# A split product's low halves moved from VectorE to GpSimd, with four re-orderings, in an attention, FFN and mixture-of-experts kernel

## The chip, the cores and the metric

The kernel runs on one core of one Trainium2 chip. The metric is the device time of one execution in microseconds (us). PE is TensorE (matmuls; PEld its weight loads), DVE is VectorE, ACT is ScalarE, POOL is GpSimd, and SP is the engine whose queue issues the DMAs.

## The reference, cut to what matters

```python
# q, k, v: [2, 8, 768, 64]: banded attention, a key is kept if it is one of the
# first 8 or at most 95 behind the query, with a bias by distance and head
a = softmax(scale * q @ k.T + bias, where=keep); attn = a @ v      # -> x [1536, 512]
h = x @ w_in                      # [512, 2048]
x = (h * sigmoid(h)) @ w_out      # [2048, 512]
e = argmax(x @ w_gate)            # 8 experts, one for each token
out = softmax(x @ w_gate)[e] * sigmoid(x @ w_output_gate)[e] * (relu(x @ w1[e]) @ w2[e])
```

## The kernel before

The 1536 tokens are 12 blocks of 128, and two blocks are a unit of 256. For exactness each FFN operand is kept as a high half, rounded to a reduced fp32 type that PE reads, and a low half, the rest; a product is three matmul groups (high by high, high by low, low by high). The weights w_in and w_out arrive as words of 64 bits, and three DVE operations on 128x512 (`decode`, L303 to L305) make fp32 of one piece. `spl_w` then takes a cast for the high half (on POOL at L326 in attention, on ACT at L327 later) and a subtraction on POOL for the low one (L333 for w_in, L339 for w_out).

**Attention first.** The first six blocks run in 24 slots of one pair of heads each (`slot_b`): scores on PE (L173), bias and minimum on DVE (L183), exponentials on ACT (L194), transposes on PE (L213), their copies pT out of PSUM (`emit_cp`, by ACT at L220 from slot DQ = 8 to slot 22, by DVE at L219 else), and products with v (L230). At the end of a block the reciprocals of its sums are spread by POOL (L1031), transposed on PE (`emit_rb`, L237), multiplied in by DVE (L242) and split by POOL (L277, L279). One decoding operation stands in each slot from 8 on: `dops` lists 15, for w_in pieces 0 to 2 and w_out pieces 0 and 1. `WPS` lists the slots behind which the five splits stand.

**Then the FFN**, in five chunks of units, `CH=[[0,1],[2],[3],[4],[5]]`, each of 16 steps over the 128-column pieces f of w_in. Chunk zero has two units. A step of it has 24 matmuls of 128x256 (L355, into two PSUM banks, one for each unit), for each unit tanh on ACT into an SBUF tile u with two buffers (L359), on DVE (u+1)*s, written back into the PSUM tile s (L360), a cast on ACT for the high half of g (L363), and on DVE the subtraction for the low half (L364), which is the last to read the bank; and then the 12 matmuls of 128x512 with w_out of two steps earlier (L375 to L377). In chunk zero each step also decodes the w_in piece of two steps later and one w_out piece, whose low half wol is first needed at L377 one step after its subtraction. From chunk one on, the other attention blocks and the gate of finished units run between the steps; the gate's pieces are a list of functions, one in each step: gate1 twice, gate2, gate3 (ranks: six small matmuls into a tile gr, L492 to L494, and DVE work on it) and gate4. The tile gr shares its PSUM bank with the transposed attention output ms (L271), which DVE reads at L279.

**Then the experts** (`moe2`). Their weights come as pieces qr by `load_u` (L578), the rows of an expert's tokens as xw by `load_x` (L688) out of the table xe, into which POOL's indirect DMAs (L515) have scattered them, all loads on SP's queue in the order of the code. ACT and DVE split qr (L583, L584); PE transposes xw (L703) and multiplies (L713, L714).

Each engine takes its instructions in the order of the code, so that a waiting one holds up all behind it.

Of the kernel before, what the change touches and what calls it, by code (L numbers as in the profile page):

```python
# [17 lines left out]
ALU = mybir.AluOpType  # L18
# [5 lines left out]
def kernel(ctx, tc, qk, v, n_global, n_local, w_in, w_out, wg, w1, w2, out):  # L24
# [3 lines left out]
    CH=[[0,1],[2],[3],[4],[5]]  # L28
    PS=bass.MemoryType.PSUM

    SB=24
    LT=3
    DQ=8
    LI=4
    LO=1
    LS=3
    WL=6
    LOPB=(1,2,3)
    WPL=(4,6,8,10,12,14,16,18,20)
    WPS=(12,14,18,22,24)  # L40
    const=ctx.enter_context(tc.tile_pool(name="const",bufs=1,side="left"))
    es_a=ExitStack(); es_m=ExitStack(); es_2=ExitStack()
    attn=es_a.enter_context(tc.tile_pool(name="attn",bufs=1,side="right"))
# [29 lines left out]
    V=nc.vector; A=nc.scalar; G=nc.gpsimd; T=nc.tensor; S=nc.sync  # L73
# [239 lines left out]
    def dec_rest():  # L313
        while half:
            k=half.pop(); r=wraw.pop(k)
            decode(wF[k],r[:,:,0],r[:,:,1],(2,),dct('a'))
    dops=[(k,st) for k in (0,2,4,1,3) for st in range(3)]
    def dec_op():
        if not dops: return
        k,st=dops.pop(0)  # L320
# [24 lines left out]
    s1p={}; gg={}; s2p={}  # L345
# [10 lines left out]
    def s1_ev(u_,f):  # L356

        t=s1p[u_,f]; u=mp.tile([P,256],F32,tag="u",name="u",bufs=2)
        A.activation(out=u,in_=t,func=AF.Tanh,scale=0.5)  # L359
        V.scalar_tensor_tensor(out=t,in0=u,scalar=1.0,in1=t,op0=ALU.add,op1=ALU.mult)  # L360
    def s1_sp(u_,f):
        t=s1p.pop((u_,f)); g=mp.tile([P,2,256],F32R,tag="g",name="g",bufs=6); gg[u_,f]=g
        A.activation(out=g[:,0],in_=t,func=AF.Copy)  # L363
        V.tensor_tensor(out=g[:,1],in0=t,in1=g[:,0],op=ALU.subtract)  # L364
    def s2_mm(c,f):
        if f==0:
            for u in CH[c]: s2p[u]=[ps.tile([P,512],F32,tag=f"s2{2*(u if c==0 else 0)+k}",name=f"s2{k}",bufs=1) for k in range(2)]
# [204 lines left out]
    def load_u(k,i):  # L572

        p,q=divmod(k,4); hf=q//2; e=ereg(p)
        r=m2['a'].tile([P,512],F32,tag="qr",name="qr",bufs=NQR); uqr[k,i]=r
        if q%2==0: src=w1[ds(e,1),i*P:(i+1)*P,hf*512:(hf+1)*512].rearrange("o p f -> p (o f)")
        else: src=w2[ds(e,1),hf*512+i*P:hf*512+(i+1)*P,:].rearrange("o p d -> p (o d)")
        S.dma_start(r,src)  # L578
# [203 lines left out]
    def moe2():  # L782
        late_split()
        early1(0,0)
        run_gates(2)
        early1(0,1)
        logits(NTT-2)
        early1(1,0)
        run_gates(1)
        late1()  # L790
        run_gates(1)
        early1(1,1)
        run_gates(1)
        early2(0)
        late3()
        order(1)
        moe2_open2()
        for k in range(NQR): load_u(4+k//4,k%4)
        load_x(1); load_t(0)
        early3(0,0)  # L800
        early2(1)
        early3(0,1); early3(1,0)
        early3(1,1)
        early4()
        atags[0]=['s1','s1b','a','pv']
        LG=2
        steps=[(p,f) for p in range(NE) for f in range(8)]
        for g in range(len(steps)+LG):
            if g<len(steps):
                p,f=steps[g]  # L810
                def spl():
                    split_u(4*(p+1)+nq[1]//4,nq[1]%4,False); nq[1]+=1
                f1_mm(p,f)
                if f!=2: folds()
                if p+1<NE and f==0: nq[:]=[0 if p else NQR,0]
                ns=(0,0,3,3,3,3,2,2)[f] if p+1<NE else 0
                f1_ev(p,f,spl if ns else lambda: None)
                if p+1==NE and 2<=f<5: flags(f-2)
                if p+1<NE:
                    for _ in range(ns-1): spl()  # L820
                    while nq[0]<min(16,nq[1]+4*(f+1),nq[1]+NQR): load_u(4*(p+1)+nq[0]//4,nq[0]%4); nq[0]+=1
                    if p and f==0: load_x(p+1)
                    if p==0 and f==5:
                        for k,s,n in tiles(0): tail(0,k,xwt[0][:,k,0:1],xwt[0][:,k,1:2])
                    t=tiles(p+1)
                    px=PX
                    if px<=f<px+len(t): prep_x(p+1,t[f-px][0])
            if g>=LG:
                p2,f2=steps[g-LG]
                if p2<NE-1:  # L830
                    f2_mm(p2,f2)
                    if f2==7: f2_ev(p2)
                    continue
                big,last=tiles(p2)
                if f2==7: f2_mm(p2,0,[big])
                f2_mm(p2,f2,[last])
                if f2==7:
                    f2_ev(p2,[last])
                    for k in range(1,8):
                        f2_mm(p2,k,[big])  # L840
                        if k==2: folds()
                    f2_ev(p2,[big])
# [148 lines left out]

    WP={}
    for k,x in enumerate(((0,0,0),(0,0,1),(0,0,2),(0,1,0),(0,1,1),(0,0,3),(0,0,4),(0,1,2),(0,0,5))): WP.setdefault(WPL[k],[]).append(x)
    for k,x in enumerate(((2,0,0),(2,0,1),(2,0,2),(2,1,0),(2,1,1))): WP.setdefault(WPS[k],[]).append(x)
    npv=[SB]; fin=[]
    TB={s:[(0,2*s-2),(0,2*s-1)] for s in range(1,5)}
    for s,hs in ((5,range(3)),(6,range(3,6)),(7,range(6,8))): TB[s]=[(2,h) for h in hs]
# [1 line left out]
    def slot_b(s):  # L999

        ev=[]
        n5,h5=divmod(s-LT-2,4); o5=0<=s-LT-2<SB
        n,hp=divmod(s,4); n1,h1=divmod(s-1,4); n3,h3=divmod(s-LT,4); n4,h4=divmod(s-LT-1,4)
        n2,h2=divmod(s-2,4); cur=s<SB; o1=0<=s-1<SB; o2=0<=s-2<SB; o3=0<=s-LT<SB; o4=0<=s-LT-1<SB
        def a_():
            if s<SB-3: want(min(s+WL,SB-1))
            elif cur: want(s+3)
            if s==0:
                m=two()
                for j in range(2): emit_qk(n,hp,j,m)  # L1010
            if cur: emit_tb(n,hp,0)
            if s+1<SB or o3: m=two()
            if o3: cp[0]=emit_tr(n3,h3,m)
            if s+1<SB:
                for j in range(2): emit_qk(*divmod(s+1,4),j,m)
            if s<3: warm(2)
            if s>=SB and o3: emit_cp(*cp[0],V)
            if o1 and s<SB: emit_exp(n1,h1)
        ev.append(a_)
        def a2():  # L1020
            if cur: emit_tb(n,hp,1)
            if o3 and s<SB: emit_cp(*cp[0],A if DQ<=s<23 else V)
            if o1 and s>=SB: emit_exp(n1,h1)
            if o4: emit_px(n4,h4)
            if o3 and h3==3 and own(n3): emit_rb(n3)
            if o4 and h4==3 and not own(n4): emit_rb(n4)
            if o5 and h5==3 and not own(n5): emit_xx(n5)
            if o2 and h2==3:
                for k in range(2): emit_rs(n2,k)
                r=attn.tile([P,512],F32,tag="t",name="rx",bufs=3)  # L1030
                G.tensor_copy(r.rearrange("p (h d) -> p h d",h=H),rs[n2].to_broadcast([P,H,D])); rs[n2]=r  # L1031
        ev.append(a2)
        def b_():
            if cur: glob_k(n,hp)
            if h4==3 and o4 and own(n4): emit_xx(n4)
            if s==0: table(slice(0,3),(1,))
            if s==1: table(slice(0,3),(2,))
            for d,h in TB.get(s,()): tab_heads(slice(0,2) if d==0 else slice(2,3),slice(0,2) if d==0 else slice(2,3),(h,))
            if hp==3 and 4*(n+1)<SB and cur: load_v(n+1)
        ev.append(b_)  # L1040
        return ev
    cp=[None]
# [41 lines left out]
    with tc.manual_schedule():  # L1084
# [13 lines left out]
        while s<SB:  # L1098
            for k,e in enumerate(slot_b(s)):
                e()  # L1100
                if k==0 and s>=DQ: dec_op()
            if s==6: rows_clear(0)
            s+=1
            for x in WP.get(s,()): w_to(*x)
# [8 lines left out]
        for g in range(len(steps)+LAG):  # L1113
# [23 lines left out]
            if g>=LAG:  # L1137
                c2,f2=steps[g-LAG]
                s2_mm(c2,f2)
                if live and g>=LAG+FB: run_gates(2 if g-(len(CH)-1)*FB in (2,4) else 1)  # L1140
                if f2==FB-1:
                    first_=[lambda u=u: s2_ev(u) for u in CH[c2]]
                    if c2==0: first_.append(lambda: (atags.__setitem__(0,['a','s22','s23']),ded.__setitem__(0,True)))
                    gq[:0]=first_
                    at=len(gq)
                    for u in CH[c2]:
                        seq=[lambda n=n,fn=turn if u in PU else gate1: fn(n) for n in (2*u,2*u+1)]
                        if u in PU: seq=[lambda u=u,fn=fn: fn(u) for fn in (piece1,piece2,piece3,piece4)]+seq+[lambda: None]*2
                        seq+=[lambda u=u,fn=fn: fn(u) for fn in (gate2,gate3,lambda u: gate4(u,1))]
                        for i,fn in enumerate(seq):  # L1150
                            if at+i<len(gq): gq[at+i]=lambda fs=(gq[at+i],fn): [f() for f in fs]
                            else: gq.append(fn)
                        at=len(gq)-(4 if u in PU else 0)
                    run_gates(3 if c2==0 else 1)
                    if c2==len(CH)-2: gq.append(lambda: order(0))
                    if c2==len(CH)-2: gq.append(moe2_open)
# [73 lines left out]
```

## Time and profile before

| | us |
|---|---|
| median of 3 runs | 565.51 (563.87 to 565.89) |
| profiled execution | 565.66 |
| its span | 563.9 |
| PE busy | 550.1 |
| DVE busy | 392.3 |
| ACT busy | 310.1 |
| POOL busy | 147.2 |

The span is what the trace covers, and 1.8 us of the profiled execution lie outside it. Attention of the first six blocks takes until about 42.6 us, chunk zero from there to about 134, the other chunks to about 362, the experts the rest. In the rows below, times count from the span's start.

### The profile page before, as it was taken

To read this page: it belongs to the slowest core of one execution; us is meant where nothing else is said; L and a number is where in the kernel's file an instruction comes from. 1 tells how busy PE (TensorE), PEld (TensorE's weight loads), DVE (VectorE), ACT (ScalarE), POOL (GpSimd) and SP (SyncE) were. 2 spreads that over 40 slices of the span, in tenths; PEclk is the share of its full clock that TensorE was granted. 3 is DMA by queue.
4 is the path that set the end of the run, shared out by engine and by line. 5 is a ranking of instruction groups with operands and counts; after the bars stand their busy time and mean duration, and the time that the engine had idled before them with its cause. 6 is when DMAs were issued, how large, how long until landed. Compare 5 with 4: busy or idle time off the path is not lost.

```text
span 563.9 us, 12050 instructions
## 1 busy us (share of the span) xinstructions
PE 550.1 (98%) x4051; PEld 467.5 (83%) x4051; DVE 392.3 (70%) x1141; ACT 310.1 (55%) x827; POOL 147.2 (26%) x201
## 2 busy tenths in 40 slices
PE   9999999999998999999999999999999999999993
PEld 4668898888887888888889889888888888888882
DVE  6996999996587767565635457647674966977950
ACT  7994344442644656444632426727655766867740
POOL 4884644344141431213101010210010110010011
PEclk9999999999999999999999999999999999999998
DMA  7886477796575765864593349319673867768500
GB/s 224 269 258 217 152 210 240 241 305 203 181 181 143 194 168 137 181 170 132 113 186 115 95 131 360 110 59 343 225 224 135 270 212 238 253 216 282 158 21 22
DMA packets 87531, 106.76 MB, mean 189 GB/s; under 512 B 35980, under 2 KB 50316, under 8 KB 87460
## 3 DMA queue, kind: packets, MB, share of 16 engines
q1 hardware_dynamic: 84980, 99.25, 59.6%
q0 software_dynamic: 2192, 6.39, 3.1%
q8 instruction: 34, 0.56, 0.4%
q14 instruction: 37, 0.30, 0.2%
q10 hardware_dynamic: 288, 0.26, 0.1%
HBM read 87.14 MB, written 17.66 MB: 186 GB/s over the span
## 4 chain that ended last, share of the span: by engine, by line
PE 87%; DVE 5%; ACT 3%; DMA 1%; POOL 1%; issue 1%; SPq 1%; POOLq 0%; ACTq 0%; DVEq 0%
PE s L355 24%; PE s L375 8%; PE s L376 7%; PE s L377 7%; PE h L713 7%; PE y L746 4%; PE h L714 4%; PE y L748 4%; PE y L747 4%; PE xy L173 3%; PE pv L254 2%; PE h L719 2%; PE y L742 2%; PE y L741 1%; PE xm L703 1%; DMA xw<-xe 1%
## 5 line engine op out<-in xcount | busy, mean ns | idle before, releaser
L355 PE MATMUL s<-xT,wi 128*128 128x256 f32 x1152 | 152.9, 284 | 0.4 <-DVE g L364 0.4
L355 PEld LDWEIGHTS s<-xT,wi 128*128 128x128 f32 x1152 | 146.5, 190 | 8.0 <-DVE g L364 3.3
L360 DVE SCALAR_TENSOR_TENSOR s<-u,s 128x256 f32<-128x256 f32 x96 | 39.8, 426 | 64.4 <-ACT u L359 64.4
L359 ACT ACTIVATE u<-s 128x256 f32<-128x256 f32 x96 | 35.3, 379 | 87.0 <-PE s L355 86.4
L375 PE MATMUL s<-woh,g 128*128 128x512 f32 x192 | 78.4, 408 | 0.0
L584 DVE TENSOR_TENSOR uq<-qr,uq 128x512 fp32r<-128x512 f32 x112 | 74.5, 689 | 3.0 <-ACT uq L583 1.0
L376 PE MATMUL s<-woh,g 128*128 128x512 f32 x192 | 75.7, 394 | 0.0
L583 ACT ACTIVATE uq<-qr 128x512 fp32r<-128x512 f32 x112 | 66.6, 625 | 0.9 <-DMA qr<-in_w_dram 0.9
L670 POOL DMA_INDIRECT out_dram<-y,ixt x17 | 18.9, 1113 | 155.2 <-ACT y L759 113.4
L364 DVE TENSOR_TENSOR g<-s,g 128x256 fp32r<-128x256 f32 x96 | 39.2, 421 | 18.3 <-ACT g L363 14.4
L363 ACT ACTIVATE g<-s 128x256 fp32r<-128x256 f32 x96 | 35.9, 380 | 28.6 <-DVE s L360 28.5
L194 ACT ACTIVATE t<-t,mx 128x256 f32<-128x256 f32 (+1 forms) x96 | 46.1, 487 | 0.5 <-DVE mx L183 0.5
L375 PEld LDWEIGHTS s<-woh,g 128*128 128x128 f32 x192 | 36.3, 189 | 6.9 <-issue 1.8
L376 PEld LDWEIGHTS s<-woh,g 128*128 128x128 f32 x192 | 36.3, 189 | 5.1
L377 PE MATMUL s<-wolr,g 128*128 128x512 f32 x128 | 39.8, 392 | 0.0
L201 POOL TENSOR_TENSOR hl<-t,hl 128x512 f16<-128x512 f32 (+1 forms) x18 | 19.5, 1085 | 75.5 <-ACT g L363 31.6
L726 DVE TENSOR_TENSOR h<-h,hs 128x192 f32<-128x192 f32 (+5 forms) x56 | 20.9, 372 | 25.3 <-ACT hs L725 25.2
L746 PE MATMUL y<-uq,hh 128*128 128x512 f32 (+1 forms) x88 | 36.7, 417 | 0.0
L747 PE MATMUL y<-uq,hh 128*128 128x512 f32 (+1 forms) x88 | 34.6, 393 | 0.0
L748 PE MATMUL y<-uq,hh 128*128 128x512 f32 (+1 forms) x88 | 34.6, 393 | 0.0
L728 ACT ACTIVATE hh<-h 128x192 fp32r<-128x192 f32 (+5 forms) x56 | 19.7, 352 | 26.4 <-DVE h L726 15.9
L731 DVE SCALAR_TENSOR_TENSOR hh<-h,hh 128x128 fp32r<-128x128 f32 (+4 forms) x88 | 23.3, 295 | 13.2 <-ACT hh L728 13.2
(279 smaller groups left out, 1065.4 us busy)
## 6 DMA issues: line engine op xcount, KB each, us to landing
qr<-in_w_dram SPq DMA_DIRECT2D x128, 256.0 KB, 4.3
wolr<-wlo_d SPq DMA_DIRECT2D x64, 256.0 KB, 3.3
wiraw<-in_w_in_dram SPq DMA_DIRECT2D x16, 512.0 KB, 4.0
wraw<-in_w_out_dram SPq DMA_DIRECT2D x13, 512.0 KB, 3.8
ring<-in_qk_dram SPq DMA_DIRECT2D x22, 256.0 KB, 4.1
xe<-xe SPq DMA_DIRECT2D x7, 792.0 KB, 6.2
wlo_d<-wol SPq DMA_DIRECT2D x16, 256.0 KB, 2.6
xw<-xe SPq DMA_DIRECT2D x15, 264.0 KB, 5.0
```

Source lines behind the costliest of these rows:

```text
L194: A.activation(out=t[:,j,:ce],in_=t[:,j,:ce],func=AF.Exp,scale=-1.0 if 4*n<SB else 0.125,bias=mx[n][:,h:h+1],accum_out=ss[n][:,h,0:1])
L355: T.matmul(t,w[:,ww,kc,:],x[:,xx,kc,:],start=(k==0),stop=(k==11)); k+=1
L360: V.scalar_tensor_tensor(out=t,in0=u,scalar=1.0,in1=t,op0=ALU.add,op1=ALU.mult)
L375: T.matmul(o,g[u][:,0,sl],wh,start=(f==0),stop=False)
L376: T.matmul(o,g[u][:,1,sl],wh,start=False,stop=False)
L377: else: T.matmul(o,g[u][:,0,sl],wl,start=False,stop=(f==FB-1))
L583: A.activation(out=t[:,0],in_=r,func=AF.Copy)
L584: (G if (i%2 if pool is None else pool) else V).tensor_tensor(out=t[:,1],in0=r,in1=t[:,0],op=ALU.subtract)
L713: for kc in range(KC): T.matmul(t[:,:2*W],uq[4*p+2*(f//4),kc][:,0,s],xwT[p,kc][:,:,:W],start=(kc==0),stop=False)
L746: T.matmul(o,hi,w[:,0],start=(f==0),stop=False)
L747: T.matmul(o,g[:,z:z+n],w[:,0],start=False,stop=False)
L748: T.matmul(o,hi,w[:,1],start=False,stop=(f==7))
```

## The change

It has four parts (line numbers of the kernel after are two to five above those of before).

1. Only the nine decoding operations of w_in pieces 0 to 2 are left in attention, in slots 8 to 18 without 11 and 15 (`DQS`), with their three splits (`WPS`). The w_out pieces 0 and 1 are decoded in steps 0 and 1 of chunk zero, as the others are. In slots 11, 15 and 20 (`CPV`) the pT copies are DVE's.
2. In chunk zero, (u+1)*s is written to the SBUF tile u in place, the cast reads it there, and the subtraction for the low half is POOL's, not DVE's. Other chunks keep what they had.
3. The ranks of unit 1 come one step later.
4. The second expert's rows xw are asked for after four of the eight qr loads.

```diff
+    DQS=(8,9,10,12,13,14,16,17,18)
+    CPV=(11,15,20)
-    WPS=(12,14,18,22,24)
+    WPS=(12,15,20)
...
-    dops=[(k,st) for k in (0,2,4,1,3) for st in range(3)]
+    dops=[(k,st) for k in (0,2,4) for st in range(3)]
...
-        V.scalar_tensor_tensor(out=t,in0=u,scalar=1.0,in1=t,op0=ALU.add,op1=ALU.mult)
+        o=u if u_ in CH[0] else t; s1p[u_,f]=o
+        V.scalar_tensor_tensor(out=o,in0=u,scalar=1.0,in1=t,op0=ALU.add,op1=ALU.mult)
...
-        V.tensor_tensor(out=g[:,1],in0=t,in1=g[:,0],op=ALU.subtract)
+        (G if u_ in CH[0] else V).tensor_tensor(out=g[:,1],in0=t,in1=g[:,0],op=ALU.subtract)
...
-        for k in range(NQR): load_u(4+k//4,k%4)
-        load_x(1); load_t(0)
+        for k in range(NQR):
+            load_u(4+k//4,k%4)
+            if k==3: load_x(1)
+        load_t(0)
...
-            if o3 and s<SB: emit_cp(*cp[0],A if DQ<=s<23 else V)
+            if o3 and s<SB: emit_cp(*cp[0],A if DQ<=s<23 and s not in CPV else V)
...
-                if k==0 and s>=DQ: dec_op()
+                if k==0 and s in DQS: dec_op()
...
-                        seq+=[lambda u=u,fn=fn: fn(u) for fn in (gate2,gate3,lambda u: gate4(u,1))]
+                        seq.append(lambda u=u: gate2(u))
+                        if u==1: seq.append(lambda: None)
+                        seq+=[lambda u=u,fn=fn: fn(u) for fn in (gate3,lambda u: gate4(u,1))]
```

On DVE, one steady step of chunk zero stands like this before: three decoding operations (dct and wt are the decoder's tiles, wraw raw w_out, wiraw raw w_in), the two units' products, the two subtractions into g, and the next decoding.

```order
L303 TENSOR_SCALAR dct<-wraw 128x512
L304 SCALAR_TENSOR_TENSOR dct<-wraw,dct 128x512
L360 SCALAR_TENSOR_TENSOR s_1493<-u,s_1493 128x256
L360 SCALAR_TENSOR_TENSOR s_1506<-u,s_1506 128x256
L364 TENSOR_TENSOR g<-s_1493,g 128x256
L364 TENSOR_TENSOR g<-s_1506,g 128x256
L305 SCALAR_TENSOR_TENSOR wt<-wraw,dct 128x512
```

And after the change:

```order
L305 TENSOR_SCALAR dct<-wraw 128x512
L306 SCALAR_TENSOR_TENSOR dct<-wraw,dct 128x512
L363 SCALAR_TENSOR_TENSOR u<-u,s_1493 128x256
L363 SCALAR_TENSOR_TENSOR u<-u,s_1506 128x256
L307 SCALAR_TENSOR_TENSOR wt<-wraw,dct 128x512
```

The two subtractions have gone, and no DVE instruction reads the bank s behind the product.

On POOL, steps 1 to 3 of chunk zero stand like this before (xT is the split of an attention block, rx the spread reciprocals, upper the first tile of the gate's constants).

```order
L277 CAST xT<-xn 128x4x128
L279 TENSOR_TENSOR xT<-xn,xT 128x4x128
L326 CAST woh<-wt 128x512
L339 TENSOR_TENSOR wol<-wt,woh 128x512
L1031 COPY rx<-rs 128x512
L333 TENSOR_TENSOR wi<-wt,wi 128x512
L277 CAST xT<-xn 128x4x128
L279 TENSOR_TENSOR xT<-xn,xT 128x4x128
L333 TENSOR_TENSOR wi<-wt,wi 128x512
L388 MEMSET upper 128x128
```

And after the change:

```order
L281 TENSOR_TENSOR xT<-xn,xT 128x4x128
L367 TENSOR_TENSOR g<-u,g 128x256 x2
L1036 COPY rx<-rs 128x512
L367 TENSOR_TENSOR g<-u,g 128x256 x2
L341 TENSOR_TENSOR wol<-wt,woh 128x512
L335 TENSOR_TENSOR wi<-wt,wi 128x512
L367 TENSOR_TENSOR g<-u,g 128x256 x2
L279 CAST xT<-xn 128x4x128
L281 TENSOR_TENSOR xT<-xn,xT 128x4x128
L341 TENSOR_TENSOR wol<-wt,woh 128x512
L335 TENSOR_TENSOR wi<-wt,wi 128x512
L391 MEMSET upper 128x128
```

Each step has got two subtractions, ahead of the weights' own, and the casts of woh have left the queue.

On PE, unit 1's ranks in chunk one stand like this before, right behind the w_out matmuls of a step and ahead of the next step's w_in matmuls (s_2145 and s_2146 are the unit's sums, geb the chosen experts).

```order
L376 MATMUL s_2146<-woh,g 128x512
L377 MATMUL s_2145<-wolr,g 128x512
L377 MATMUL s_2146<-wolr,g 128x512
L492 LDWEIGHTS upper
L492 MATMUL gr<-geb,upper 128x8
```

And after the change:

```order
L379 MATMUL s_2146<-woh,g 128x512
L380 MATMUL s_2145<-wolr,g 128x512
L380 MATMUL s_2146<-wolr,g 128x512
L357 MATMUL s_2694<-xT,wi 128x256 x12
L175 MATMUL xy<-ring_76 128x256 x4
```

The w_in matmuls follow directly, and the ranks come behind that step's own w_out matmuls.

## Rows read from the trace of the kernel before

**Rows 1.** The page: PE's busy time, the chain by engine, one group of instructions.
```profile
PE 550.1 (98%) x4051; PEld 467.5 (83%) x4051; DVE 392.3 (70%) x1141; ACT 310.1 (55%) x827; POOL 147.2 (26%) x201
PE 87%; DVE 5%; ACT 3%; DMA 1%; POOL 1%; issue 1%; SPq 1%; POOLq 0%; ACTq 0%; DVEq 0%
...
L364 DVE TENSOR_TENSOR g<-s,g 128x256 fp32r<-128x256 f32 x96 | 39.2, 421 | 18.3 <-ACT g L363 14.4
```

**Rows 2.** Chain of waits, 59 to 138 us: w_in matmuls (start, us, what).
```profile
59.72 2.87 PE s L355 x24
65.34 2.87 PE s L355 x24
...
93.43 3.05 PE s L355 x24
...
134.31 1.43 PE s L355 x12
```

**Rows 3.** Waits, 42.6 to 138 us: total us, times, longest.
```profile
PEld s L355 <- DVE g L364: 3.3, 8, 0.7
```

**Rows 4.** Timeline of one step (start, us, engine, line, tiles; [idle before <- releaser]).
```profile
118.35 1.30 POOL L339 TENSOR_TENSOR wol<-wt,woh 128x512 fp32r<-128x512 f32 x1 [2.30 <-ACT woh L327]
...
119.17 0.69 DVE L305 SCALAR_TENSOR_TENSOR wt<-wiraw,dct 128x512 int32<-128x512 int32 x1
...
121.22 0.75 DVE L360 SCALAR_TENSOR_TENSOR s<-u,s 128x256 f32<-128x256 f32 x2
...
122.10 0.76 DVE L364 TENSOR_TENSOR g<-s,g 128x256 fp32r<-128x256 f32 x2
122.58 0.19 PEld L355 LDWEIGHTS s<-xT,wi 128*128 128x128 f32 x1 [0.39 <-DVE g L364]
```

**Rows 5.** Busy time by stretch, PE, PEld, DVE, ACT, POOL; clock, DMA, GB/s.
```profile
23.50:30.00 6.50, 6.50 (x88) 4.22 (x86) 6.20 (x25) 6.50 (x27) 6.18 (x9) 1.00 1.00 337
...
93.40:134.30 40.90, 40.90 (x255) 35.62 (x255) 37.22 (x69) 17.21 (x41) 17.13 (x14) 1.00 0.82 264
```

**Rows 6.** Timeline of PE, start of chunk zero's third step.
```profile
53.05 3.13 PE L355 MATMUL s<-xT,wi 128*128 128x256 f32 x24 [0.42 <-DVE g L364]
```

**Rows 7.** Timeline of POOL, steps 2 to 4 of chunk zero.
```profile
58.72 0.61 POOL L277 CAST xT<-xn 128x512 fp32r<-128x512 f32 x1 [1.25 <-DVE xn L242]
...
62.75 0.21 POOL L388 MEMSET upper<- 128x128 bf16 x1
...
65.98 1.30 POOL L339 TENSOR_TENSOR wol<-wt,woh 128x512 fp32r<-128x512 f32 x1
```

**Rows 8.** Timeline of POOL and DVE: subtractions in chunk one.
```profile
163.03 0.69 POOL L201 TENSOR_TENSOR hl<-t,hl 128x256 f16<-128x256 f32 x1
...
166.63 1.53 DVE L201 TENSOR_TENSOR hl<-t,hl 128x512 f16<-128x512 f32 x1
```

**Rows 9.** Timeline of PE and DVE around unit 1's ranks.
```profile
180.10 0.68 DVE L279 TENSOR_TENSOR xT<-ms,xT 128x512 fp32r<-128x512 f32 x1
...
180.84 0.17 PE L492 MATMUL gr<-geb,upper 128*128 128x8 bf16 x1 [1.67 <-DVE xT L279]
...
187.82 0.43 DVE L360 SCALAR_TENSOR_TENSOR s<-u,s 128x256 f32<-128x256 f32 x1 [2.14 <-ACT u L359]
```

**Rows 10.** Timeline of POOL, SP's queue and PE where the second expert begins.
```profile
377.32 0.97 POOL L515 DMA_INDIRECT xe<-xr,gdi  x1 [2.04 <-DMA xe<-xr,gdi]
378.37 4.45 SPq L578 DMA_DIRECT2D qr<-in_w_dram  x8
383.34 2.00 SPq L688 DMA_DIRECT2D xw<-xe  x3
...
389.46 0.63 PE L703 MATMUL xm<-ident,xw 128*128 128x128 f32 x4 [0.45 <-DMA xw<-xe]
```

**Rows 11.** Timeline of attention: a pair of pT copies, and PE's wait for POOL.
```profile
34.49 0.68 ACT L220 ACTIVATE pT<-xy 128x256 f32<-128x256 f32 x2
...
41.05 0.42 PEld L237 LDWEIGHTS rb<-ident,rx 128*128 128x128 f32 x4 [0.37 <-POOL rx L1031]
```

More of the change, by code (lines that the diff above doesn't have):

```diff
@@ L993 @@
     for k,x in enumerate(((0,0,0),(0,0,1),(0,0,2),(0,1,0),(0,1,1),(0,0,3),(0,0,4),(0,1,2),(0,0,5))): WP.setdefault(WPL[k],[]).append(x)
-    for k,x in enumerate(((2,0,0),(2,0,1),(2,0,2),(2,1,0),(2,1,1))): WP.setdefault(WPS[k],[]).append(x)
+    for k,x in enumerate(((2,0,0),(2,0,1),(2,0,2))): WP.setdefault(WPS[k],[]).append(x)
     npv=[SB]; fin=[]
```

## The prediction, made before the result was known

> **What bounds the kernel now.** I read the page's busy times and the chain of waits first. PE is busy 550.1 us of the span's 563.9 and is 87% of the chain [rows 1]. Its clock is granted in full, 1.00, which is the level of 2.4 GHz [rows 5]. So nothing can be won but PE's gaps, at most 563.9 - 550.1 = 13.8 us, and each part of the change has to be set against the gap that it is aimed at. The other engines cost only where one of them makes PE wait.
>
> The longest stretch of such gaps is chunk zero. Along the chain, a step (from one start of the 24 w_in matmuls to the next) takes 65.34 - 59.72 = 5.62 us at first, but from 93.43 on the seven steps to 134.31 take 40.88, that is 5.84 each [rows 2]. The waits of that stretch name one releaser, the DVE subtraction L364: 3.3 us in 8 waits of PE's loads [rows 3]. The timeline of one late step shows it directly: DVE runs the products, then the subtractions from 122.10, and PE's next load starts as they end the first bank, having stood for 0.39 [rows 4]. DVE is busy 37.22 of 40.90 us there [rows 5], and the rest is gaps of a few hundredths between its instructions. A step's DVE work is six decoding operations of 0.69, two products (0.75) and two subtractions (0.76) [rows 4], 5.65 us, or 5.84 with the gaps: DVE is the bound by two tenths of a microsecond in each step, and falls behind until PE's lead is used up at 93.43.
>
> **Part 2, chunk zero: the sum's first two terms.** The subtractions leave DVE, 0.76 in a step, and it has 5.84 - 0.76 = 5.1 us of work in PE's 5.62. The bank is free once the product has been written to u, earlier than before by cast and subtraction. So steps should run at PE's own 5.62: 13 x 5.62 = 73.1 against 134.31 - 59.72 = 74.6 us, **1.5 us won**. The third step's start at 53.05 waits 0.42 for the same subtraction [rows 6]; that should go too: **0.4 won**.
>
> What the six decoding operations of w_out add in steps 0 and 1 (6 x 0.69 = 4.1 us on DVE) lies in the first three steps, where DVE loses the subtractions of 0.76 in each and has gaps; their low halves come in the same pattern as piece 2's, a step before use. I cost that at nothing.
>
> The new work is 32 subtractions on POOL. No row has this form exactly. The nearest is POOL's own subtraction of a 128x256 tile, 0.69 [rows 8], with an f16 result; from above bounds the 128x512 one of 1.30 [rows 4], from below half of it, 0.65. I take 0.69, the same size. POOL then has 1.30 + 1.30 (the weights' two) + 2 x 0.69 = 4.0 us in a step of 5.62. The cast reading SBUF rather than PSUM is ACT's, which is busy 17.21 of 40.90 [rows 5]: nothing.
>
> The new wait is tanh's: u has two buffers, POOL reads them last, and behind a waiting tanh on ACT stand the casts, on which DVE's and POOL's work and then PE hang. In a steady step POOL is done with u by about 4.5 us into the step, and the next tanh comes at 5.62 + 1.4: slack 2.5. The tight place is the gate's constants on POOL, from 62.75 to the start of L339 at 65.98, 3.2 us [rows 7]. I follow POOL by the new order from step 2, in estimates from these durations. Its two subtractions end at about 58.9, close to where the attention block's cast starts now, 58.72; that cast and its subtraction (0.61 + 1.30) end at 60.8, the two weights' (2.6) at 63.4, the constants at 66.6, step 3's subtractions (1.4) at 68.0, and the low half of w_out piece 2 at 69.3. PE needs that last one in step 4, behind 24 w_in matmuls and eight with w_out: step 3 starts at 59.72 - 0.42 = 59.3, and 59.3 + 5.62 + 2.87 is 67.8; the twelve w_out matmuls share 5.62 - 2.87 = 2.75, eight of them 1.8, so 69.6. The margin is 0.3 us; tanh of step 4 waits about 1 us, PE does not, and POOL has caught up two steps later. So I cost it at nothing, narrowly.
>
> Here a rule speaks against the part. The row has POOL at 0.69 for the size. The Trainium skill, "GPSIMD Engine Reference", section "4.1 Engine selection", says that elementwise work belongs on VectorE and that GpSimd is about twice as slow with two inputs. By that, an estimate from the rule and the 0.42 mean of DVE's subtraction [rows 1] would be 0.84, the low half would be 4 x 0.15 - 0.3 = 0.3 late, once, and the whole sum 3.9 where it is 4.2 by the row.
>
> **Part 3, ranks of unit 1.** PE waits 1.67 us at 180.84 because the ranks' tile shares a bank with the transposed block that DVE reads at L279, 180.10 to 180.78 [rows 9]. One step later the bank has long been read; the w_in matmuls, which need nothing of it, go first. The six small matmuls cost the same wherever they stand. DVE's work on the ranks then waits at its queue's head for PE; behind it stands the next product, before which DVE has 2.14 idle [rows 9], more than the few short operations take. What is late next would be the pT tiles of that stretch, which DMA transposes bring behind DVE's own splits and which PE needs a step later; I reckon a few tenths to spare. **1.7 won**, and as little as nothing if PE meets these instead (rival B).
>
> **Part 4, rows of the second expert.** PE waits 0.45 for xw at 389.46 [rows 10]. Eight qr loads ahead of it take SP 4.45, 0.56 each; four fewer bring xw 2.2 us sooner, past the need. The rows must lie in xe by then: the last scatter runs to 377.32 + 0.97, and the one before kept POOL waiting for 2.04 until it had landed [rows 10], so by about 380.3, and xw would now be asked for at 383.34 - 2.2 = 381.1. The four qr loads that now stand behind come 2.0 later [rows 10]; by its order ACT takes their pieces only after that, and should it wait, at most those 2.0 less its lead are lost. **0.5 won**.
>
> **Part 1, attention.** In the stretch shown ACT is full (6.50 of 6.50), and so is PE [rows 5]. Three pairs of pT copies, 0.68 for two that overlap [rows 11], leave ACT, some 2 us, for DVE, in slots in which DVE loses a decoding operation of 0.69. So ACT's relief is 2 us at the most, but PE shows next to no gap there into which it could go, and near the end it is the block's way over POOL that sets the time: PE waits 0.37 for it at 41.05 [rows 11]. In the new order that way's first step, L242, stands behind two pairs of copies on DVE, about where it begins now. I take **0.1 won**, a part of that one gap; the range is from 0.4 lost (the gap twice as long) to 0.8 won (near half of ACT's relief reaches PE, rival C).
>
> **Sum.** 1.5 + 0.4 + 1.7 + 0.5 + 0.1 = 4.2 us. Against the profiled execution, 565.66 - 4.2 = 561.4. The median of the runs is 565.51, 0.15 lower, so 561.3 us.
>
> **The rivals.**
> *A. POOL is late once, at the constants (563.9).* PE's waits for L364 go as reckoned, but POOL's subtraction costs near its upper bound. At 1.29 a POOL step is 5.2, still under 5.62, but at the constants four subtractions are each 0.6 longer: 2.4 less the margin of 0.3, and half a microsecond from the step before, some 2.6 us late once. 561.3 + 2.6 = 563.9. For it: no row has the fp32r result with this size. Against: the 128x512 form with that result is 1.30, twice 0.65, so size and not type sets it.
> *B. The ranks' wait is replaced (562.9).* If the transposes or another DVE product come as late as the bank did, part 3 gives nothing or little, and 561.3 + 1.6 = 562.9. For it: chunk one is the place where DVE, SP and PE are all close. Against: after the waits of that step DVE has 2.14 idle.
> *C. Attention gains more (560.5).* If the three copies shorten the whole way from slot 11 on, 0.6 to 0.8 more. For it: ACT is busy without a gap. Against: the wait for POOL.
> *D. Slower: POOL becomes chunk zero's bound (570.1).* DVE's subtraction L201 took 1.53 in a stretch in which POOL worked too [rows 8], where DVE's subtraction of that size at L279 took 0.68 [rows 9]: 0.85 more. If POOL's subtractions lose as much beside DVE's steady work, they cost 0.69 + 0.85 = 1.54 to 1.30 + 0.85 = 2.15; in the middle, 1.85, a POOL step is 2.6 + 3.7 = 6.3, and 13 steps take 81.9 rather than 73.1: 561.3 + 8.8 = 570.1. It decides from (5.62 + 0.32 - 2.6) / 2 = 1.67 each, where the loss in 13 steps eats the 4.2. Against: POOL's 1.30 at 118.35 ran beside DVE's L305 at 119.17, and both took what they take elsewhere [rows 4]. The Trainium skill, "SBUF — State Buffer", section "SBUF: two separate sides", has the two engines lock each other out only when DVE has two SBUF inputs or a two-port mode; L201 has two, and no DVE operation of chunk zero has, so by that page D does not come.
> *E. Part 2's gaps hide another bound,* as the weights' splits that now stand behind the subtractions on POOL: then the steps stay at 5.84, and 1.5 + 0.4 are lost, 563.2.
>
> **How the numbers follow.** Forecast 0.57 (560.8 to 562.0), A 0.12, B 0.11, C 0.09, E 0.06, D 0.05. The range takes in C and, above, B, E and A: 559.9 to 564.0, leaving out D and the tails. A measurement of this kernel tells about 0.5% (2.8 us) from no change: faster means under 562.7, slower over 568.3. Faster: the forecast with C, 0.66, and the milder half of B and the mildest of A, 0.07, make 0.73. Same: the rest of A and B with E, 0.22. Slower: D, 0.05.
>
> **What the profile after would show.** Steps of chunk zero at 5.62 throughout, no wait of PE for L364 or its POOL successor, and 128x256 subtractions on POOL of about 0.7; tanh waiting for POOL about 1 us in step 4 alone; no wait ahead of the ranks, and none in place of it at the next pv; xm without a wait; attention's end within half a microsecond of 42.6. I am wrong if POOL's subtraction is well over 0.8, if PE waits for wol in step 4, or if the 1.7 us return elsewhere in chunk one.

## The result: slower, 571.84 us

The changed kernel takes 571.84 us (median of 4 runs, 570.56 to 572.41) where the kernel before takes 565.06 (median of 4): 1.0118 times as long, interval 1.0092 to 1.0145, some 6.7 us. The prediction was 561.3, with 559.9 to 564.0 as its range; it is wrong in sign.

The page of the kernel after, its busy times and the engines of its chain:

```profile
PE 551.8 (97%) x4051; PEld 469.8 (82%) x4051; DVE 385.1 (68%) x1115; ACT 312.1 (55%) x823; POOL 168.7 (30%) x231
...
PE 81%; DMA 5%; DVE 5%; ACT 2%; POOL 2%; SPq 2%; issue 2%; POOLq 0%; DVEq 0%; ACTq 0%
```

Against [rows 1] DVE has given work to POOL as planned, and yet PE's share of the chain has fallen from 87% to 81%, while DMA's, POOL's and SP's queue's, 1% each before, have grown. Of DMA's 5%, 1% is wgs; 3% are qr loads in the chain between 340 and 400 us. What is new for PE, the waits from 60 to 85 us of the kernel after say (engine, line, what it waited for: us, times, longest):

```profile
PEld s L380 <- POOL wol L341: 6.4, 1, 6.4
PE s L380 <- POOL wol L341: 6.0, 1, 6.0
POOL wgb L405 <- DMA wgs<-in_wg_dram: 5.9, 1, 5.9
```

One stall, in step 4 of chunk zero. POOL stood 5.9 us for wgs, the gate's weights, and PE stood 6.0 for the low half wol that POOL makes behind it. The chain of waits of that stretch shows the whole way (start, us, what):

```profile
61.34 1.26 POOL wol L341
62.60 0.02 issue
62.62 0.33 SPq L343
...
62.99 0.93 SPq L416
...
63.97 0.61 SPq L291
...
64.63 0.50 SPq L295
...
65.17 6.42 DMA wgs<-in_wg_dram
...
72.92 1.41 POOL g L367 x2
74.33 1.23 POOL wol L341
...
75.60 2.07 PE s L380 x4
77.67 4.44 PE s L357 x24
...
84.87 2.87 PE s L357 x24
```

It is read from the top: POOL finishes the low half of w_out piece 1, and only then can SP issue its write to DRAM (L343). Behind that write, on SP's queue, stand a clearing of xe (L416), two raw weights (L291, L295), and then wgs at 65.17, which lands 6.42 later. Before the change the same queue stood like this (timeline of SP, kernel before):

```profile
42.94 0.33 SPq L341 DMA_DIRECT2D wlo_d<-wol  x1
...
47.53 0.33 SPq L341 DMA_DIRECT2D wlo_d<-wol  x1
...
52.10 0.55 SPq L400 DMA_DIRECT2D wgs<-in_wg_dram  x1
```

and after it (timeline of SP, kernel after):

```profile
55.54 0.33 SPq L343 DMA_DIRECT2D wlo_d<-wol  x1
...
62.62 0.33 SPq L343 DMA_DIRECT2D wlo_d<-wol  x1
...
65.17 0.64 SPq L403 DMA_DIRECT2D wgs<-in_wg_dram  x1
```

The two writes are 12.6 and 15.1 us later because w_out pieces 0 and 1 are decoded and split later, and wgs, whose place in the code hasn't changed, is 13.1 us later. Before, POOL read it first 12.6 us after its issue, and did not wait (timeline of POOL, kernel before):

```profile
64.71 0.24 POOL L402 CAST wgb<-wgs 128x64 bf16<-128x64 f32 x1
```

Little of those 12.6 us was to spare. When it landed the trace of before doesn't show; in those of parts 2 and 3, each alone, where SP's queue is in the order of before, wgs landed 9.6 and 9.2 after its issue, 1.6 and 3.6 us ahead of POOL's first reading.

The last rows of the chain show a second price. Four w_out matmuls take 2.07 where they take 0.91 elsewhere, and 24 w_in matmuls 4.44 for 2.87: 2.7 us more. The stretches of busy time of the kernel after name it (PE, PEld, DVE, ACT, POOL, then the granted clock):

```profile
69.00:72.00 3.00, 0.58 (x3) 0.15 (x1) 0.00 (x0) 0.00 (x0) 0.26 (x2) 1.00 0.52 166
...
77.70:79.00 1.30, 1.30 (x8) 1.30 (x8) 1.16 (x3) 0.45 (x1) 1.30 (x2) 0.50 0.96 321
...
82.20:85.00 2.80, 2.80 (x15) 2.35 (x14) 2.30 (x4) 1.74 (x4) 2.02 (x3) 1.00 0.42 124
```

PE had been idle for 6 us, and came back at a granted clock of 0.50, the 1.2 GHz level, until about 81.1. So the stall cost 6.0 + 2.7 = 8.7 us.

By stages of the two traces: the stretch from the first w_in matmul of chunk zero to the first of chunk one is 91.6 us before (42.69 to 134.31) and 98.2 after (42.90 to 141.07), so 6.6 more, that is 8.7 lost and about 2.2 won. From there to the first eh matmul, which opens the experts, 0.7 is won: 1.8 at the ranks, where PE no longer waits, less 1.1 at the end of chunk four, where ACT stood 0.5 for a late qr; of the other profiles only that of parts 2 and 3 alone loses as much as 0.7 there. From there to the last yf matmul, the last product of the experts, 0.2 is lost.

### The profile page after: what moved, and what is told of

Its sections match the earlier page's. It is cut to its first block, busy times and chain, and to the rows that moved or that the text cites. A ratio compares the mean times of both kernels' runs of the same rounds, so it can differ in the third digit from the quotient of the medians.

```text
span 570.3 us, 12053 instructions
## 1 busy us (share of the span) xinstructions
PE 551.8 (97%) x4051; PEld 469.8 (82%) x4051; DVE 385.1 (68%) x1115; ACT 312.1 (55%) x823; POOL 168.7 (30%) x231
## 4 chain that ended last, share of the span: by engine, by line
PE 81%; DMA 5%; DVE 5%; ACT 2%; POOL 2%; SPq 2%; issue 2%; POOLq 0%; DVEq 0%; ACTq 0%
PE s L357 20%; PE s L378 6%; PE h L716 6%; PE s L380 6%; PE s L379 6%; PE y L749 4%; PE xy L175 4%; PE y L750 4%; PE y L751 4%; PE h L717 4%; DMA qr<-in_w_dram 3%; PE pv L256 2%; PE h L722 2%; PE px L232 2%; PE y L745 1%
## 5 line engine op out<-in xcount | busy, mean ns | idle before, releaser
L357 PEld LDWEIGHTS s<-xT,wi 128*128 128x128 f32 x1152 | 148.9, 193 | 5.4 <-issue 0.3
L363 DVE SCALAR_TENSOR_TENSOR s<-u,s 128x256 f32<-128x256 f32 x64 | 27.3, 426 | 56.0 <-ACT u L361 55.9
L367 DVE TENSOR_TENSOR g<-s,g 128x256 fp32r<-128x256 f32 x64 | 27.0, 421 | 16.6 <-ACT g L366 14.8
L366 ACT ACTIVATE g<-s 128x256 fp32r<-128x256 f32 x64 | 24.3, 380 | 22.6 <-DVE s L363 22.5
L716 PE MATMUL h<-xwT,uq 128*128 128x448 f32 (+5 forms) x144 | 32.5, 347 | 0.0
```

The lines of the kernel that those rows point to most:

```text
L357: T.matmul(t,w[:,ww,kc,:],x[:,xx,kc,:],start=(k==0),stop=(k==11)); k+=1
L716: for kc in range(KC): T.matmul(t[:,:2*W],uq[4*p+2*(f//4),kc][:,0,s],xwT[p,kc][:,:,:W],start=(kc==0),stop=False)
```

## The experiments

Theory Q, after the result: SP stands for the moved writes, wgs is late, POOL's queue stands for wgs, PE for wol. Rival P: POOL, with the new subtractions, could not have brought wol in time in any case, and the wgs wait only fills time that POOL's load would have cost. All comparisons are with the kernel before on the same chip, where it took 565.6 to 565.8. The first four expectations count from the 565.06 above, so that they stand 0.6 too low.

**Wgs loaded early.** The whole change, with one DMA moved from step 3 of chunk zero into attention's slot 20:

```diff
-        S.dma_start(wgs,wg.rearrange("(k p) e -> p k e",p=P))
...
             if s==6: rows_clear(0)
+            if s==20: S.dma_start(wgs,wg.rearrange("(k p) e -> p k e",p=P))
```

> The whole change, but the load of the gate's weights wgs is issued in attention's slot 20, ahead of the two wol writes on SP's queue, not at step 3 of chunk zero. Theory Q (queue): the loss is SP standing for the moved wol writes, so that wgs lands late (71.6 us), POOL stands 5.9 us for it at the gate's constants and PE 6.0 us for wol of piece 2 behind that, with the clock down afterwards (2.7 us). Then POOL no longer waits for wgs, PE waits at most 0.3 us for wol in step 4, the clock stays at 1.00, and the time is 565.1 - 1.5 - 0.4 - 1.7 = 561.5 us, 561.0 to 562.3. Rival P (POOL's load): with the new subtractions POOL cannot bring wol in time after the constants anyway. Then PE still waits 2 us or more in step 4, and the time is 563.5 to 567 us.

Measured: 563.05 us, 0.9955 times before (0.9939 to 0.9971), 2.6 us faster. One 32 KB transfer issued earlier turns the change from 1.2% slower to 0.45% faster. Its chain in steps 3 to 6:

```profile
59.40 2.87 PE s L357 x24
...
65.02 2.89 PE s L357 x24
67.91 0.72 POOL g L367
68.63 1.26 POOL wol L341
...
69.93 1.21 PE s L380 x4
71.14 2.87 PE s L357 x24
...
76.76 2.87 PE s L357 x24
```

A wait of 0.2 us for wol is left (step 4 takes 71.14 - 65.02 = 6.12, half a microsecond over 5.62), all other steps from 3 on are at 5.62. P expected 2 us or more, so Q holds, with P true to half a microsecond: this is the narrow place that the prediction followed on POOL. The time lies 0.8 above Q's range: 0.6 of that is the base, the rest less than step 4's half microsecond.

**Part 1 alone** (the decoding moved, three pT copies on DVE, subtractions still on DVE):

```diff
+    DQS=(8,9,10,12,13,14,16,17,18)
+    CPV=(11,15,20)
-    WPS=(12,14,18,22,24)
+    WPS=(12,15,20)
...
-    dops=[(k,st) for k in (0,2,4,1,3) for st in range(3)]
+    dops=[(k,st) for k in (0,2,4) for st in range(3)]
...
```

> Part 1 alone (w_out pieces 0 and 1 decoded in chunk zero, three pT copies on DVE); the subtractions stay on DVE. Q: the wol writes are late on SP here too, wgs lands at about 71 us, POOL stands for it about 6 us, and wol of piece 2 comes one POOL subtraction (1.3 us) later at about 74; PE waits 4 to 5 us for it and runs at half clock for some 4 us, 2.7 us: 565.1 + 4.5 + 2.7, less up to 1.5 that DVE gains back while PE stands: 570.8 us, 569.5 to 572.5. P: no new subtraction on POOL, so no stall: 565 us, 564.3 to 565.8.

Measured: 574.26 us, 1.0154 (1.0132 to 1.0176). The stall is here without any new work on POOL (waits, 60 to 85 us):

```profile
POOL wgb L404 <- DMA wgs<-in_wg_dram: 5.3, 1, 5.3
...
PE s L379 <- POOL wol L341: 4.6, 1, 4.6
```

So part 1 makes the stall by itself, which P can't explain. The time is above Q's range by 1.8 us, 0.6 of it the base; besides, at the ranks of unit 1, which this kernel still has a step early, PE waits 1.7 and then comes back at a lower clock, which costs 1.5 and of which more below.

**Part 1 alone, wgs early**, to take the stall away from it:

```diff
...
-        S.dma_start(wgs,wg.rearrange("(k p) e -> p k e",p=P))
...
+            if s==20: S.dma_start(wgs,wg.rearrange("(k p) e -> p k e",p=P))
```

> Part 1 alone with wgs loaded early. Q: the stall of part 1 alone goes (no wait of PE for wol over 0.5 us in step 4, clock 1.00): 8 us less than part 1 alone, 565.9 us (564.8 to 566.8). Rival: the late writes and reads of wol themselves hold PE up: 568 us or more.

Measured: 569.28 us, 1.0066 (1.0047 to 1.0085). The wait for wol is gone, but not all of the loss. The time is the rival's, 2.5 above Q's range, but not for the rival's reason: PE waits for no wol or wolr in chunk zero. The chain of chunk zero shows the first part of the loss:

```profile
59.72 2.87 PE s L357 x24
65.33 3.02 PE s L357 x24
71.10 3.10 PE s L357 x24
76.95 3.10 PE s L357 x24
```

From 65.33 on the 24 matmuls take more than 2.87, and the steps go to 5.85; before, this began only at 93.43 [rows 2]. With the six decoding operations, 4.1 us of work, DVE's lead is used up five steps sooner, and chunk zero takes 1.1 us more. Alone, part 1 is a loss; only without the subtractions on DVE is it hidden. Another 1.5 us lie behind unit 1's ranks, again with a lower clock.

**Part 2 alone** (product into u, subtraction on POOL):

```diff
...
+        o=u if u_ in CH[0] else t; s1p[u_,f]=o
...
+        (G if u_ in CH[0] else V).tensor_tensor(out=g[:,1],in0=t,in1=g[:,0],op=ALU.subtract)
```

> Part 2 alone (product to SBUF, the low halves' subtraction on POOL in chunk zero); w_out pieces 0 and 1 decoded in attention as before, so SP's queue is as before. Q: wgs is there in time (issued at about 52), no PE wait in step 4 over 0.3 us, steps of chunk zero at 5.62, 128x256 subtractions of 0.7 on POOL: 565.1 - 1.9 = 563.2 us, 562.6 to 564.0. P: PE waits about 2 us in step 4: 565 us or more.

Measured: 564.47 us, 0.9984 (0.9968 to 1.0000): 0.9 us won by the ratio, 0 to 1.8, in the forecast's range only with the base put right. P's mechanism isn't there, as PE has no wait in step 4. In its trace chunk zero takes 89.4 us (42.07 to 131.49) and not 91.6: 2.2 won there, a little over the 1.9 forecast. What is missing in its time is seen at the ranks (stretches with the granted clock, as above, and PE's timeline):

```profile
177.00:178.70 1.70, 0.28 (x7) 0.28 (x7) 1.36 (x5) 0.13 (x2) 1.15 (x1) 1.00 0.84 269
178.70:180.00 1.30, 1.30 (x8) 1.30 (x8) 1.02 (x8) 0.21 (x1) 0.00 (x0) 0.55 0.29 78
180.00:181.50 1.50, 1.50 (x8) 1.27 (x9) 0.33 (x1) 0.13 (x1) 0.48 (x2) 0.50 1.02 195
```
```profile
178.41 0.17 PE L493 MATMUL gr<-geb,upper 128*128 128x8 bf16 x1 [1.67 <-DVE xT L279]
...
178.57 2.70 PE L355 MATMUL s<-xT,wi 128*128 128x256 f32 x12
181.20 1.62 PE L173 MATMUL xy<-ring 64*128 64x256 f32 x8
```

The same place in the kernel before:

```profile
179.00:180.90 1.90, 0.23 (x4) 0.15 (x4) 1.75 (x7) 0.55 (x2) 1.06 (x1) 1.00 0.75 222
180.90:182.50 1.60, 1.60 (x18) 1.55 (x17) 1.09 (x8) 0.21 (x1) 0.09 (x1) 1.00 0.45 130
```

The wait is the 1.67 us of [rows 9], but after it the clock is at 0.50, and the next matmuls take 2.70 and 1.62 where in the kernel before they take 1.66 and 1.13. In the traces of this kernel, of part 1 alone and of part 1 with wgs early, the step behind the ranks takes 6.2 to 6.3 us where it took 4.7: 1.5 us more. In the kernel before the clock stays at 1.00 over the same wait, and in part 4 alone over one of 1.18.

**Part 3 alone** (unit 1's ranks a step later):

```diff
...
+                        if u==1: seq.append(lambda: None)
...
```

> Part 3 alone (ranks of unit 1 one step later). As forecast: no wait of PE at the ranks, none in its place: 565.1 - 1.7 = 563.4 us, 562.9 to 564.0. Rival: another wait takes its place at the next products with v: 564.5 to 565.5 us.

Measured: 564.20 us, 0.9978 (0.9965 to 0.9991), 1.3 us won by time (0.5 to 2.0), between the forecast's range and the rival's, and in the forecast's with the base put right. In the trace the wait is gone, and from chunk one's first w_in matmul to the first eh it takes 225.9 us, before 227.9. But a new wait has come, at a product with v, as the rival had it, a quarter as long (timeline of PE):

```profile
197.19 0.76 PE L254 MATMUL pv<-vpr,pT 128*128 128x64 bf16 x20 [0.43 <-DMA pT<-hl]
```

The other profiles with part 3 have at most 0.3 there, that of the whole change under 0.1. Nor is the 2.0 a measure by itself: the trace of part 4 alone, whose code is the same up to the experts, has a wait of 1.18 at the ranks, and their step takes 5.5 us in it, where it takes 6.3 in the kernel before and 4.0 here.

**Part 4 alone** (the second expert's rows after four loads):

```diff
...
+            if k==3: load_x(1)
...
```

> Part 4 alone (the second expert's rows after four qr loads). As forecast: no wait of PE at xm and none in its place, 0.5 us won: 565.2 us where the kernel before takes 565.65; from the first eh matmul to the last yf one 188.0 us, before 188.5. Rival (a new wait takes its place): the four qr loads that now stand behind land later, ACT stands for them, its split of xw comes late and PE waits 0.3 us or more for it: nothing won, 565.5 to 566.0, that stretch 188.5 to 188.8.

Measured: 566.50 us, 1.0013 (0.9998 to 1.0028): nothing won. The rival's mechanism holds; the time is 0.5 above its range. The trace, of the fastest of the 12 runs (563.62), has no wait at xm, the transposes of xw, but these (timeline, 380 to 405 us):

```profile
386.32 1.28 ACT L583 ACTIVATE uq<-qr 128x512 fp32r<-128x512 f32 x2 [0.59 <-DMA qr<-in_w_dram]
...
396.27 2.06 PE L719 MATMUL h<-xwT,uq 128*128 128x272 f32 x12 [0.41 <-ACT xwT L705]
```

ACT now stands 0.59 for a qr that has been put behind xw, and its split of xw comes late enough for PE to wait 0.41, as long as the 0.45 that was saved. All profiles with part 4 have this wait, 0.3 to 0.7, and none without it; there, in five of seven, PE waits 0.3 to 0.8 at xm.

**Parts 1 to 3 with wgs early, without part 4:**

```diff
...
-        for k in range(NQR):
-            load_u(4+k//4,k%4)
-            if k==3: load_x(1)
-        load_t(0)
+        for k in range(NQR): load_u(4+k//4,k%4)
+        load_x(1); load_t(0)
...
```

> Parts 1, 2 and 3 with wgs loaded early, without part 4. If part 4 wins 0.5 us: 0.5 us above the kernel with all four parts and wgs early. If it wins nothing or costs 0.2: equal to that or 0.2 below it, 562.8 us; the stretch from eh to yf is 188.5 us.

Measured: 562.12 us, 0.9938 (0.9921 to 0.9955), 0.9 below the same with part 4, though the two intervals meet. The wait at xm is back, with 0.6, and none comes after it. From the first eh to the last yf it takes 188.6 us, and with part 4 it took 188.8: the traces don't show where 0.9 would lie. **Parts 2 and 3 alone,** with the decoding where it was, take as long, 0.3 above the range expected of them:

> Parts 2 and 3 alone: decoding as before, wgs where it was. Theory Q with the traces so far (attention under part 1 takes 0.3 us more from its first reciprocals' transposes to chunk zero, and with part 1 wol of piece 2 comes 0.5 us late even with wgs early): PE has no wait in step 4, steps of 5.62, no wait at the ranks: 565.65 - 1.9 - 1.7 to 2.5 = 561.3 to 562.0 us, 0.8 below parts 1 to 3 with wgs early. If part 1 were worth its forecast 0.1 or more: not below that kernel.

Measured: 562.28 us, 0.9940 (0.9921 to 0.9960). So part 1, with its queue put right, shows neither gain nor loss beside parts 2 and 3, and the expected 0.8 us between them isn't there, where each interval leaves about 1 us either way. This trace has no wait in chunk zero but one of 1.1 us for a wolr load in chunk one, in no other profile over 0.1; whether it belongs to the kernel is open.

**Which link of the queue?** Two kernels with the whole change leave the load of wgs where it is. In one the two writes are issued behind it:

```diff
+            if f<2: wlw.append((f,l))
+            else: S.dma_start(wlo_d[f],l.bitcast(F32))
...
+                    if g==3: atags[0]=['a']; gate_consts(); [S.dma_start(wlo_d[f_],l_.bitcast(F32)) for f_,l_ in wlw]
```

> The whole change, wgs loaded in its place at step 3, but the two writes of wol 0 and 1 to DRAM stand on SP's queue behind the load of wgs instead of ahead of it. Theory Q: it is SP standing for the finished wol that makes wgs late; then wgs is issued before 60 us, POOL does not wait for it, PE waits 0.3 us or less in step 4, and the time is that of the kernel with wgs early, 563.0 us (562.2 to 563.8). Rival: something else of the moved decoding holds SP (a raw buffer that is freed later): wgs still lands after 66 us, PE stands 2 us or more, 566 us or more.

Measured: 563.69 us, 0.9967 (0.9948 to 0.9986), as with wgs early, and chunk zero takes 89.8 us as there. SP now issues wgs first and stands afterwards (its timeline):

```profile
43.68 0.90 SPq L404 DMA_DIRECT2D wgs<-in_wg_dram  x1
56.44 7.42 SPq L1131 DMA_DIRECT2D wlo_d<-wol  x2
```

In the other wgs stays late, but POOL's four operations that read it stand in step 6:

```diff
+    def gate_consts2():
...
+                if g==6: gate_consts2()
```

> The whole change with the late wgs load as it is, but the four POOL operations that read wgs stand in step 6, not at the head of POOL's queue in step 3. Theory Q: what stops PE is POOL's queue standing for wgs; so with wgs just as late (about 71.6 us) POOL goes on to the subtractions and wol, the wait of PE in step 4 is gone (even the 0.2 us that is left with wgs early, since 1.2 us of the constants have moved), and the time is 562.6 us (561.8 to 563.6). Rival: SP's late queue hurts PE by another way too (the raw weights loaded behind it): a wait of PE in steps 4 to 8 of 1 us or more, 564 us or more.

Measured: 563.21 us, 0.9946 (0.9925 to 0.9967). Wgs is as late as in the changed kernel,

```profile
66.19 0.63 SPq L403 DMA_DIRECT2D wgs<-in_wg_dram  x1
```

and nobody waits: POOL goes past it, PE has no wait in steps 3 to 15, and the 0.2 us for wol is gone too, since 1.2 us of the constants have moved. So the harm was in the head of POOL's queue, and SP's lateness by itself costs PE nothing. The same **without part 4:**

> The same without part 4. If part 4 costs what the pair before showed (0.3 to 0.9 us): 561.7 to 562.3 us; if it costs nothing: 562.6 us as the kernel beside it.

Measured: 562.62 us, 0.9930 (0.9907 to 0.9953), 0.6 below its pair, again within the intervals. It is the time expected if part 4 costs nothing, but its pair came 0.6 above the time expected too. In all three comparisons the kernel with part 4 is slower, by 0.6 to 0.9 us, and in none is that clear of noise: part 4 wins nothing, and that it costs something isn't shown. The three kernels without the stall and without part 4 (562.1 to 562.6) beat the kernel before by 0.6% to 0.7%, clear of noise.

## Why the prediction was wrong, point by point

- **The failed step** is the sentence on part 1's six decoding operations, "I cost that at nothing". It counted their DVE time and the moment at which their low halves are needed, but not the write to DRAM that each split issues on SP. That queue is in order: raw weights and in the end wgs stood behind the writes. wgs was issued 13.1 us later, where 12.6 had lain between its issue and its use, and landing alone takes 9.2 and 9.6 in two traces with the old queue; POOL stood 5.9 us for it, PE 6.0 for POOL, and the lower clock took 2.7 more: 8.7 us for a term put at nothing.
- **POOL's narrow place** was the right place with the wrong cause. The prediction named "if PE waits for wol in step 4" as a sign of being wrong, and the sign came. It followed POOL step by step and took the constants' 3.2 us as POOL's own work. In [rows 7] they were so, because wgs was there; that they wait for a load wasn't asked. With wgs early this working came true to half a microsecond: tanh waits 1.1 us, wol is 0.2 late where a margin of 0.3 was reckoned.
- **The price of POOL's subtraction** was nearly right: 0.74 for one, 1.41 to 1.45 for two that follow each other, against 0.69. The Trainium skill, "GPSIMD Engine Reference", section "4.1 Engine selection", has GpSimd at about twice VectorE's time with two inputs, an estimate of 0.84 from DVE's mean of 0.42; the measured ratio is 1.8.
- **Chunk zero's gains** were right, and a little low: steps at 5.62, 2.2 us in the trace of part 2 alone against 1.5 + 0.4. The 0.3 more lies at the start of the third step too: with the wait of 0.42 the matmuls behind it also follow their predecessors more closely, on the chain 2.87 for 3.13.
- **The ranks** were right in mechanism: 1.7 forecast, 1.8 in the trace of the whole change, 1.3 (0.5 to 2.0) by the time of part 3 alone, where a wait of 0.43 at a product with v took the place of some of it. That the wait can cost another 1.5 us by the clock wasn't seen.
- **Attention** was not settled: from the first reciprocals' transposes to chunk zero it takes 26.9 to 27.6 us in the profiles with part 1, and 26.6 to 27.2 in those without. A gain of 0.1 isn't there to be seen, a loss of some 0.3 is likely, not shown.
- **Part 4** was wrong: 0.5 forecast, nothing found. The prediction named ACT's wait for the later qr and priced it at none without a row for when ACT needs them.
- **Rival D** gave 570.1, near the result, by a mechanism that isn't there: POOL's subtractions took 0.72 to 0.75 beside DVE's work, not 1.85. Its nearness is luck. No case in the prediction held the cause.

The sum put right for the profiled kernel: 2.2 and 1.8 won, 8.7 lost by the stall, 1.1 at chunk four's end, 0.6 elsewhere: the 6.4 us between the spans.

## What to carry to other kernels

Of a step that is moved, write down every queue on which it puts an instruction, and for each of them the next thing that somebody waits for; a store that waits for a late producer holds all loads behind it on an in-order queue, however small they are. An engine's burst of small work should be looked at for a load in it, and what reads a load shouldn't stand at the head of a queue on which the bottleneck's operands are made. A load put ahead of others takes its time from those, so ask when each of these is needed before calling it free.

## What the runs showed of the hardware

- After 6.0 and 4.6 us of idling (the change, part 1 alone), and in three traces after 1.7 us, PE's granted clock was 0.50, the 1.2 GHz level, for the next 3 to 6 us of its work; the stall of 6.0 us cost 8.7, those of 1.7 up to 3.2. Over the same 1.7 us the trace of the kernel before kept 1.00. What decides between them is open.
- The 32 KB load of wgs took 6.4 us from its issue to its landing in the changed kernel, with three larger transfers issued in the 2.2 us before it; 9.2 and 9.6 in parts 3 and 2 alone, with six in the 4.2 us before it; 4.7 with wgs early.
